# The opening of an FFT-and-MLP kernel: second twiddle table from two short series, bias parts made on eight partitions, weight loads first, three PSUM tiles for stage X

## The chip, the cores and the metric

The kernel runs on one core of one Trainium2 chip. The metric is device time in microseconds (us), as a median of several runs. The engines are TensorE (PE, with its weight loads shown as PEld), VectorE (DVE), ScalarE (ACT), GpSimd (POOL) and SyncE (SP), which issues most DMAs. POOL issues some DMAs as well. In the profile, queue q0 holds the DMAs that POOL issues and q1 those that SP issues.

## The reference

The input x has shape (8, 3008, 256). Each batch goes through a real FFT along the sequence, a complex linear layer with bias, a soft threshold, and the inverse FFT. The result goes through an MLP with an ELU.

```python
X = np.fft.rfft(x, axis=1)
Yr = Xr @ w_r - Xi @ w_i + b_r
Yi = Xr @ w_i + Xi @ w_r + b_i
Yr = np.sign(Yr) * np.maximum(np.abs(Yr) - 0.01, 0.0)      # the same for Yi
y = np.fft.irfft(Yr + 1j * Yi, n=3008, axis=1)
h = y.reshape(8 * 3008, 256) @ moe_w_in                    # 256 -> 2048
g = np.where(h > 0.0, h, np.exp(np.minimum(h, 0.0)) - 1.0)
out = g @ moe_w_out                                        # 2048 -> 256
```

## The kernel before

The FFT length is split as 3008 = 47 x 64. Each batch passes five stages on TensorE:

- A (`unit_A`, L129): six units, each the product of table M1 with 512 KB of x; the results are cast to bf16 and written to a DRAM buffer DA, because the next stage needs another layout.
- X (`unit_X`, L166): Z is loaded from DA in four pieces of eight rows (`load_Z`, L159). Eight units, two for each piece of Z, multiply with table M2. Each unit's result is copied ("evacuated") from PSUM to XT by `evac` (L123), on ACT (L127) or DVE (L125).
- M (`m_group`, L185): XT times the weights wcat_r and wcat_s. Half of batch 0's groups (`first_M` with on_act, L220) add the bias with one more matmul, of ones (busy) and bias_p. Rows 0, 32 and 64 of bias_p hold the bias as three bf16 parts that add up to its fp32 value. The other groups add bias_bc on DVE (L202) and are clipped on POOL (L230, L231).
- B (`unit_B`, L233) and Y (`unit_Y`, L274): the inverse, with tables M3 and M4, through a DRAM buffer DB, whose content comes back as Bs (`load_Bs`).

Batch 0 runs through these stages alone. From then on the MLP runs in a loop over blocks (`front` and `back`; L716 and L774 are its two products) with the stages of the next batches spread through it by `plan` (L801).

The tables M1 to M4 are computed on the chip, in the opening, beside stage A of batch 0. The order of instructions is written out by hand (`tc.manual_schedule()`), and each engine, and each DMA queue's issuer, works through its own list in order.

M2 holds cosines and sines of angles for 32 slots s of 2 x 24 columns on 96 partitions. The kernel before makes it in four groups g of eight slots (384 elements on each partition): `points` (L429) reduces integers mi to sample points kv and their half sign st; `phases` (L445) scales the points to angles v2; `wraps` (L460) takes the nearest integer away; `sizes` (L472) takes the absolute value on ACT; `signs` (L466) forms the second argument; `sines` (L476) is the Sin on ACT. `slot0` (L482) corrects slot 0.

The bias parts are made in place: six small DMAs put the two bias rows three times each into brow (L304), and full-width instructions on ACT and DVE split them (L601 to L610).

The weights w_r and w_i are loaded by SP after stage A's writes (L518, L519), and POOL arranges them in wcat_r and wcat_s, one part negated (L520 to L523). On SP the four Z loads, two loads of bias_bc (L527) and the first piece of w_in (L578) follow.

x for batch 0 comes in six loads (`first_x`, L314), issued by POOL between its iotas. `gate` (L585) is a small POOL copy that holds POOL until a piece of Z has landed, so that the loads of batch 1's x (L116) start only then.

`idle_pe(n)` (L295) issues n filler matmuls into a PSUM tile of their own (ips, L298): nine at the start, three between the A units, forty ahead of X, one after each X unit.

[...] In the opening pre2 has two tiles of two banks, used by A, X and B, pre1 three of one bank for M, and pre0 one for the fillers.

The functions that the change touches, and their callers:

## Time and profile before

| what | us |
|---|---|
| median of 3 runs | 912.17 (911.17 to 912.38) |
| the profiled execution | 911.1 |
| its span | 909.3 |
| first A matmul / last A matmul starts | 5.98 / 13.22 |
| last evacuation of A ends on ACT | 14.97 |
| Z is issued | 18.26 |
| first X matmul starts | 22.62 |
| last X evacuation ends | 30.69 |
| batch 1's first A matmul starts | 46.99 |
| first MLP product (L716) starts | 56.89 |

Times inside the execution count from the start of the span. The page of the profile gives each engine's busy time and a chain: the work that ended last, followed back through whatever released each step. The timeline lists instructions by start, duration, engine, line and operation; in brackets stands the idle time before and what ended it. The view of waits adds up who waited for whom. The DMA view counts the packets, bytes and busy share of each queue in a stretch of time. For the share, 100% is all 16 DMA engines busy.

### The profile page before, as it was taken

How to read it: one execution, taken by the hardware profiler on the slowest of the kernel's cores; microseconds unless marked ns; L12 is line 12 of the kernel's file. 1: busy time of each engine (PE TensorE's matmuls, PEld its weight loads, DVE VectorE, ACT ScalarE, POOL GpSimd, SP SyncE). 2: the span in 40 equal slices, each digit the busy share in tenths (PEclk: the TensorE clock that was granted, in tenths of full speed). 3: DMA queues.
4: the chain of work that ended last, by engine and by line, in shares of the span. 5: the costliest groups of instructions: out<-in, count | busy, mean ns of one | idle time of the engine just before them, and what ended most of it. 6: DMA issues, size and time to landing. Idle time of an engine off the chain costs nothing.

```text
span 909.3 us, 17183 instructions
## 1 busy us (share of the span) xinstructions
PE 887.7 (98%) x6622; PEld 652.0 (72%) x6726; DVE 717.0 (79%) x891; ACT 696.6 (77%) x851; POOL 314.7 (35%) x440
## 2 busy tenths in 40 slices
PE   8889999999999999999999999999999999999997
PEld 3457667876688677886678766787667866777775
DVE  8768778877788778797788877888778877778776
ACT  6668788777878778787787788878887877767664
POOL 7600540333321441405404153033332134443664
PEclk9999999999999999999999999999999999999999
DMA  8997116621283215732166032752228111231011
GB/s 270 309 265 232 47 48 186 209 70 47 83 236 123 71 47 142 192 109 82 58 196 199 24 98 60 207 171 70 70 70 232 29 43 47 79 86 48 24 48 47
DMA packets 90670, 106.24 MB, mean 117 GB/s; under 512 B 5270, under 2 KB 81308, under 8 KB 87228
## 3 DMA queue, kind: packets, MB, share of 16 engines
q1 hardware_dynamic: 84332, 77.62, 30.7%
q0 software_dynamic: 5968, 27.26, 9.1%
q8 instruction: 52, 0.85, 0.4%
q14 instruction: 30, 0.25, 0.1%
q10 hardware_dynamic: 288, 0.26, 0.1%
HBM read 55.32 MB, written 49.81 MB: 116 GB/s over the span
## 4 chain that ended last, share of the span: by engine, by line
PE 85%; DVE 5%; ACT 4%; DMA 3%; issue 2%; SPq 1%; POOL 0%; DVEq 0%; ACTq 0%; POOLq 0%
PE ps_o L774 34%; PE hps L716 33%; PE mps L192 9%; PE yps L282 2%; PE bps L244 2%; PE aps L144 2%; PE xps L175 2%; DMA Bs<-DB 2%; DVE gT L743 1%; DVE Et L755 1%; ACT Et L730 1%; ACT Et L727 1%; ACT Bz L257 1%; DVE osb L785 1%; SPq L792 0%
## 5 line engine op out<-in xcount | busy, mean ns | idle before, releaser
L774 PE MATMUL ps_o<-w_out_r,gT 128*128 128x256 f32 x3008 | 477.1, 301 | 0.2 <-DVE gT L741 0.2
L774 PEld LDWEIGHTS ps_o<-w_out_r,gT 128*128 128x128 f32 x3008 | 403.4, 189 | 50.3 <-DVE osb L785 1.3
L716 PE MATMUL hps<-yT,w_in_s 128*128 128x512 bf16 (+7 forms) x1650 | 382.1, 351 | 6.3 <-DVE gT L743 0.9
L741 DVE SCALAR_TENSOR_TENSOR gT<-Et,hps 128x512 fp32r<-128x512 f32 (+1 forms) x274 | 224.0, 847 | 75.8 <-POOL Et L753 38.8
L743 DVE SCALAR_TENSOR_TENSOR gT<-hps,Et 128x1024 fp32r<-128x1024 f32 x197 | 240.9, 1223 | 16.6 <-PE hps L716 1.4
L716 PEld LDWEIGHTS <-w_in_s 128*128 128x128 bf16 x1728 | 141.6, 98 | 129.0 <-issue 22.0
L730 ACT ACTIVATE Et<-hps 128x1024 f32<-128x1024 f32 x197 | 203.0, 1030 | 11.9 <-PE hps L716 5.4
L753 POOL TENSOR_SCALAR Et<-Et 128x512 f32<-128x512 f32 x189 | 112.5, 613 | 221.4 <-ACT Et L725 221.4
L755 DVE TENSOR_SCALAR Et<-Et 128x1024 f32<-128x1024 f32 x197 | 136.2, 691 | 47.4 <-ACT Et L730 40.5
L210 POOL TENSOR_SCALAR clip<-yb 128x512 f32<-128x512 f32 x84 | 51.6, 614 | 315.4 <-DVE yb L202 277.9
L725 ACT ACTIVATE Et<-hps 128x512 f32<-128x512 f32 x190 | 103.2, 595 | 64.7 <-PE hps L716 63.9
L727 ACT ACTIVATE Et<-hps 128x1024 f32<-128x1024 f32 x84 | 86.2, 1026 | 71.7 <-PE hps L716 70.1
L211 POOL TENSOR_TENSOR Y<-yb,clip 128x512 bf16<-128x512 f32 x84 | 107.2, 1276 | 7.0
L728 ACT ACTIVATE Et<-Et 128x1024 f32<-128x1024 f32 x84 | 88.8, 1058 | 2.7
L202 DVE TENSOR_TENSOR yb<-mps,bias_bc 128x512 f32<-128x512 f32 x89 | 61.3, 689 | 35.8 <-PE mps L192 23.9
L127 ACT CAST XT<-xps 128x768 bf16<-128x768 f32 x61 | 48.7, 799 | 16.2 <-PE xps L175 16.2
L127 ACT CAST yT<-yps 128x752 bf16<-128x752 f32 x63 | 49.7, 788 | 13.4 <-PE yps L282 13.3
L192 PE MATMUL mps<-wcat_r,XT 128*128 128x512 bf16 x180 | 55.6, 384 | 0.8 <-ACT Bz L257 0.3
L192 PE MATMUL mps<-wcat_s,XT 128*128 128x512 bf16 x182 | 54.9, 379 | 0.7
L127 ACT CAST A<-aps 128x1024 bf16<-128x1024 f32 x43 | 43.5, 1014 | 13.0 <-PE aps L144 12.3
L192 PEld LDWEIGHTS <-XT 128*128 128x128 bf16 x384 | 30.8, 98 | 29.6 <-DVE XT L125 0.6
L257 ACT CAST Bz<-bps 128x1024 bf16<-128x1024 f32 x46 | 46.0, 999 | 2.1 <-PE bps L244 2.1
(112 smaller groups left out, 413.5 us busy)
## 6 DMA issues: line engine op xcount, KB each, us to landing
xt<-in_x_dram POOLq DMA_DIRECT2D x21, 1024.0 KB, 7.2
out_dram<-osb SPq DMA_DIRECT2D x158, 128.0 KB
Bs<-DB SPq DMA_DIRECT2D x32, 384.0 KB
DB<-Bz SPq DMA_DIRECT2D x21, 512.0 KB
DA<-A SPq DMA_DIRECT2D x19, 512.0 KB
Z<-DA SPq DMA_DIRECT2D x7, 1152.0 KB
Z<-DA SPq DMA_DIRECT2D x11, 384.0 KB
xt<-in_x_dram POOLq DMA_DIRECT2D x6, 512.0 KB, 5.8
```

The source lines that it names most:

```text
L127: nc.scalar.copy(dst, src)
L192: nc.tensor.matmul(ps, lhsT=XT[:, dt, c, o : o + P], rhs=wm[:, dt, :], start=(not biased and m == 0 and dt == 0), stop=(m == 1 and dt == 1),)
L211: nc.gpsimd.tensor_tensor(Y_of[b, q][:, i, :], yb, clip[:], ALU.subtract)
L716: nc.tensor.matmul(hps[:, s, c0:c1], lhsT=w_in_s[:, dt, ft * P : ft * P + P], rhs=yT_of[b][:, dt, t0 : t0 + c1 - c0], start=(dt == 0), sto ...
L725: nc.scalar.activation(E_[:, s], hps[:, s], AF.Exp)
L727: nc.scalar.activation(E_, hps[:], AF.Relu, scale=-1.0)
L730: nc.scalar.activation(E_, hps[:], AF.Exp)
L741: nc.vector.scalar_tensor_tensor(o, e, -1.0, h, ALU.add, ALU.max)
L743: nc.vector.scalar_tensor_tensor(o, h, 0.0, e, ALU.max, ALU.add)
L753: eng.tensor_scalar(E_[:, s], E_[:, s], 1.0, 0.0, ALU.min, ALU.max)
L755: nc.vector.tensor_scalar(E_, E_, 1.0, -1.0, ALU.min, ALU.add)
L774: nc.tensor.matmul(po[q][:, i_ % 2, :], lhsT=gT[:, s, i_ * P : i_ * P + P], rhs=w_out_r[:, ft, :], start=(ft == 0 and i_ % 2 == 0), stop=( ...
```

## The change

It has four parts, all in the opening.

1. M2's angles. The integer points and their scaling are replaced by sums: a short series over the slots (sp, 32 elements) and a table over 78 offsets (tab). The table is read through a sliding window (`window`), which steps backward over the slots. A second table, tsg, gives the signs through the same window. `wraps` becomes one instruction, since a sum lies within one turn of the wanted range. The work goes in two halves of 16 slots, and slot 0's extra row reads tab directly. All sums and wraps stand ahead of stage A's evacuations on DVE, `sizes` and the first `sines` after unit 3 on ACT, `signs` after unit 5.
2. Bias parts. The bias is loaded as 8 x 64 by two DMAs and split by five small DVE instructions (`split_bias`) after the signs. The three parts are written to a DRAM buffer bias_d, ahead of the Z loads on SP, and read back into rows 0, 32 and 64 of bias_p, behind bias_bc. POOL clears bias_p early.
3. Weights and x. The loads of w_r and w_i become SP's first, and x's first load POOL's first. The negated part of wcat_s is made on ACT after the Sines. Unit 4 of stage A is emptied by DVE; unit 5 half by ACT and half by DVE, with a write for each half.
4. Stage X. It gets a pool of three two-bank PSUM tiles, closed before M; pre2 and pre1 are opened after it. DVE empties five of the eight units, ACT three; Abs and the two Sin of M3 go on ACT between them. The first M group takes both products of XT's first half before those of the second. The gate for batch 1's x waits for Z's fourth piece instead of its second. Fillers: 7 at the start instead of 9, 34 before X instead of 40, one after every other X unit.

```diff
@@ pools
-    pre2 = first.enter_context(tc.tile_pool(name="pre2", bufs=2, space=bass.MemoryType.PSUM))
-    pre1 = first.enter_context(tc.tile_pool(name="pre1", bufs=3, space=bass.MemoryType.PSUM))
     pre0 = first.enter_context(tc.tile_pool(name="pre0", bufs=1, space=bass.MemoryType.PSUM))
+    sooner = ExitStack()
+    pre2 = sooner.enter_context(tc.tile_pool(name="preX", bufs=3, space=bass.MemoryType.PSUM))
@@ unit_A
+        j0 = 8 * ci
+        if alone and u == 5:
+            for j in range(2):
+                c = 4 * uu + 2 * j
+                evac(A[:, c : c + 2, :].rearrange("p n d -> p (n d)"), ps[:, j, :], bool(j))
+                nc.sync.dma_start(dav[:, j0 + c : j0 + c + 2, :], A[:, c : c + 2, :])
+            return
@@ m_group
+        for n_ in range(4):
+            c, dt = (n_ % 2, n_ // 2) if (b, q, i) == (0, 0, 0) else (n_ // 2, n_ % 2)
...
@@ start
-    nc.vector.memset(brow[:], 0.0)
-    for o, bv in ((0, b_r), (D, b_i)):
-        for k in range(3):
-            nc.sync.dma_start(
-                brow[32 * k : 32 * k + 1, o : o + D],
...
-    idle_pe(9)
+    BR, BC = 8, 2 * D // 8
+    bpart = wk3.tile([BR, 3, BC], BF16, name="yb", tag="yb")
+    bias_d = dram.tile([3, BR, BC], BF16, name="bias_d", tag="bias_d")
...
+    first_x(0)
+    idle_pe(7)
+    def split_bias():
+        nc.vector.tensor_copy(bpart[:, 0], brow[:])
+        nc.vector.tensor_tensor(rest[:], brow[:], bpart[:, 0], ALU.subtract)
+        nc.vector.tensor_copy(bpart[:, 1], rest[:])
+        nc.vector.tensor_tensor(rest[:], rest[:], bpart[:, 1], ALU.subtract)
+        nc.vector.tensor_copy(bpart[:, 2], rest[:])
...
+        nc.sync.dma_start(w_r_f[:], w_r.rearrange("(c p) e -> p c e", p=P))
+        nc.sync.dma_start(w_i_f[:], w_i.rearrange("(c p) e -> p c e", p=P))
+        for o, bv in ((0, b_r), (BR // 2, b_i)):
+            nc.sync.dma_start(
+                brow[o : o + BR // 2, :],
...
@@ tables
+        def window(t, s0, ns, c, b):
+            return bass.AP(
+                tensor=t.tensor, offset=t[0:RZ, TD - s0 : TD - s0 + 1].offset,
+                ap=[t[0:RZ].ap[0], [-1, ns], [1 - 2 * c, K1]],
+            )
+        def short_tables():
+            dve.tensor_scalar(tmp[:], trow, 36.0 / N1, CMAGIC, ALU.mult, ALU.add)
...
+            dve.tensor_scalar(tsg[:], tji[:], NS + 0.5, -0.5, ALU.is_gt, ALU.add)
+        def sums(s0, s1):
+            for c in range(2):
+                dve.tensor_tensor(
+                    kt(v2, s0, s1)[:, :, :, c],
+                    sp[z, s0:s1].unsqueeze(2).to_broadcast([RZ, s1 - s0, K1]),
+                    window(tab, s0, s1 - s0, c, None), ALU.add,
+                )
...
+        def wraps(s0, s1):
+            v = v2[z, s0:s1]
+            dve.scalar_tensor_tensor(v, v, 0.5, v, ALU.is_gt, ALU.subtract)
+        def signs(s0, s1):
+            for c in range(2):
+                a = kt(a2, s0, s1)[:, :, :, c]
                 dve.scalar_tensor_tensor(
+                    a, a, qd[z], window(tsg, s0, s1 - s0, c, None), ALU.subtract, ALU.mult
                 )
@@ order
+            unit_A(0, u, alone=True, on_dve=u == 4)
...
+        short_tables()
+        sums(0, 16)
+        wraps(0, 16)
+        sums(16, 32)
+        wraps(16, 32)
+        for u in range(6):
             fA(u)
+            if u == 3:
+                sizes(0, 16)
+                sizes(16, 32)
+                sines(0, 16, 0)
+        signs(0, 16)
+        signs(16, 32)
+        split_bias()
+        nc.sync.dma_start(bias_d.rearrange("k r c -> r k c"), bpart[:])
         for g in range(4):
             load_Z(0, 8 * g, 8 * g + 8)
...
+        for k in range(3):
+            nc.sync.dma_start(
+                bias_p[32 * k : 32 * k + 1, :], bias_d[k : k + 1].rearrange("k r c -> k (r c)")
+            )
+        pool.tensor_copy(wcat_r[:, :, 0:D], w_r_f[:])
+        pool.tensor_copy(wcat_r[:, :, D : 2 * D], w_i_f[:])
+        pool.tensor_copy(wcat_s[:, :, D : 2 * D], w_r_f[:])
+        sines(16, 32, 0)
+        sines(0, 16, 1)
+        sines(16, 32, 1)
+        slot0()
+        nc.scalar.activation(wcat_s[:, :, 0:D], w_i_f[:], AF.Copy, scale=-1.0)
...
-        idle_pe(40)
+        idle_pe(34)
+        for u in range(8):
+            unit_X(0, u, alone=True, on_dve=u not in (0, 3, 6))
+            if u == 0:
+                nc.scalar.activation(a3[:], w3[:], AF.Abs)
+            if u in (3, 6):
+                o, src, sc, bi = ((1, w3, TURN, 0.0), (0, a3, -TURN, hpi[:]))[u // 6]
...
+            if u % 2 == 0:
+                idle_pe(1)
@@ after X
-    gate(Z_of[0][:, 8, 0:1])
+    gate(Z_of[0][:, 24, 0:1])
...
+    sooner.close()
+    pre2 = first.enter_context(
+        tc.tile_pool(name="pre2", bufs=2, space=bass.MemoryType.PSUM, reuse_waits="tile")
+    )
+    pre1 = first.enter_context(
+        tc.tile_pool(name="pre1", bufs=3, space=bass.MemoryType.PSUM, reuse_waits="tile")
+    )
```

## The prediction

> **What bounds the kernel now.** The page's engine table and chain come first: over the whole span TensorE is the bound.

> ```profile
> PE 887.7 (98%) x6622; PEld 652.0 (72%) x6726; DVE 717.0 (79%) x891; ACT 696.6 (77%) x851; POOL 314.7 (35%) x440
> PE 85%; DVE 5%; ACT 4%; DMA 3%; issue 2%; SPq 1%; POOL 0%; DVEq 0%; ACTq 0%; POOLq 0%
> ```

> The diff touches only work ahead of the first weight product, about the first 31 us of 909.3, where TensorE mostly runs filler (ips). So the question is when stage M of batch 0 can start. From there to 47 us the chain is nearly all TensorE, and what follows moves along with it. The chain of waits around that point:

> ```profile
> 24.93 0.88 DVE XT L125
> 25.80 0.04 issue
> 25.85 0.51 PE xps L175 x8
> ...
> 29.72 0.97 DVE XT L125
> 30.69 0.05 issue
> 30.73 0.82 PE mps L192 x3
> ```

> Stage M starts at 30.73, when DVE has emptied the last X unit. Two things set that: when Z arrives, and how fast eight X units pass two PSUM buffers. The latter is slow because DVE, which takes three of them, also splits the bias (timeline, DVE):

> ```profile
> 23.83 1.10 DVE L602 TENSOR_TENSOR yb<-yb,bias_p 128x512 f32<-128x512 f32 x1
> 24.85 0.94 DVE L125 CAST XT<-xps 128x768 bf16<-128x768 f32 x1
> 25.83 0.42 DVE L607 CAST bias_p<-yb 32x512 bf16<-32x512 f32 x1
> 26.26 0.42 DVE L608 CAST bias_p<-yb 64x512 bf16<-64x512 f32 x1
> 26.71 0.69 DVE L609 TENSOR_TENSOR yb<-yb,bias_p 64x512 f32<-64x512 f32 x1
> 27.44 0.69 DVE L610 CAST bias_p<-yb 64x512 bf16<-64x512 f32 x1
> ```

> Ahead of X lie transfers. The DMA view of 7.75 to 11.25 us shows x (q0) alone on the DMA engines, though three DA writes had been issued; from 11.25 to 17 the DA writes (q1) follow:

> ```profile
> q0 software_dynamic: 349, 1.26, 110.1%
> ...
> q1 hardware_dynamic: 3145, 1.57, 93.2%
> ```

> (packets, MB, share.) All six x loads land in turn and each stage-A pair of matmuls starts at a landing: 5.98, 7.16, 8.97, 10.37, 11.63, 13.22. Z is issued at 18.26, when the last DA write has landed (SP's waits, then its timeline):

> ```profile
> SPq L164 <- DMA DA<-A: 1.6, 1, 1.6
> ...
> 15.41 0.54 SPq L518 DMA_DIRECT2D w_r_f<-in_w_r_dram  x1
> 15.99 0.49 SPq L519 DMA_DIRECT2D w_i_f<-in_w_i_dram  x1
> 18.26 1.74 SPq L164 DMA_DIRECT2D Z<-DA  x4
> ```

> Counting 4 KB packets in windows of 0.25 us, Z's 384 are done at about 25.9; x landings came 0.55 to 1.05 after their last packets, so the last piece lands 8.2 to 8.7 us after Z's issue.

> **Weights first.** The w loads leave the place behind the DA writes and go out at about 0.75, when SP is released, instead of 15.41. Their 0.52 MB took 1.3 us at the rate of 17.25 to 18.55. That now lies ahead of x. In return x's first load goes out 0.65 sooner (1.47 now, behind five small POOL instructions) and the w packets fill part of the slow start (2.75 to 4.25). Bounds for x5: 0.65 earlier if the weights are free, 0.65 later if nothing overlaps; I take 0.3 later, since 1.3 us of data against 0.65 plus some start-up is nearer to the second. M1 keeps its time: DVE waited for the 0.48 memset, now gone, about as long as pcol is now pushed back by the load. Seven fillers instead of nine at the start cost nothing: x0 is awaited.

> **Second table.** Now DVE makes points, phases, wraps and signs in 384-element pieces, some 0.35 to 0.6 each, ending at 21.1, and POOL writes mi (0.91 + 0.83 + 1.0). After: nine small DVE instructions of 78 or fewer elements (0.25 each, from the 64-element rows of 0.21 to 0.28), four sums (0.55, L434), two 768-element wraps (0.9, L600), ready at about 12.2. What counts is the tail. After evacuation 3 (ends 12.12 now, 12.4 with the shift) ACT does two Abs and a Sin of 768 before it empties half of unit 5: three steps of 0.75 (the pitch of L613), so that half starts at 14.55 and ends at 15.15 (0.59, L254). DVE empties the other half, behind it; the one such split in this trace runs in series:

> ```profile
> 47.09 0.59 ACT L254 CAST A<-bps 128x512 bf16<-128x512 f32 x1 [0.31 <-PE bps L244]
> 47.71 0.69 DVE L255 CAST A<-bps 128x512 bf16<-128x512 f32 x1 [1.10 <-ACT A L254]
> ```

> So DVE is done at 15.86, 0.9 later than ACT is now (14.97). Behind that on DVE stand four signs (0.53, the pitch of L468): 17.95; then five instructions of split_bias (8x64; 0.22 by the 128x64 rows): 19.05.

> **Bias parts.** The new write to bias_d stands ahead of Z on SP and waits for split_bias. With 0.35 for its issue, Z goes out at 19.4, 1.15 later than now. The DA landing, the wait that ends last today, comes at about 18.5 (17.0 data end, 0.3 shift, 1.2 to land), so it loses its place to the new wait. Bounds of Z's issue: 18.5, the DA landing alone; 20.4, with x 0.65 later and small instructions at 0.3. I take 19.4, since it is a sum of rows of the same shapes.
> In return 3.3 us of DVE (L602 to L610) and 0.6 of ACT leave stage X, and 0.48 of memset the start. The three bias_p loads queue behind Z and bias_bc; they land by about 29 and are wanted at E + 0.5 (E: the end of the last X evacuation).

> **Three buffers and the M3 sines.** Evacuations go 5 to DVE (0.9 pitch) and 3 to ACT (0.8); Abs and two Sin (0.84, 0.85, 0.92) fit between. X alone would need 5.7 us against 8.1 now. Z's last piece, at 19.4 + 8.4 = 27.8, ends later than that pace from Z's first, landed by some 23.6 (23.6 + 5.7 = 29.3 against E below). From 27.8: 0.57 to the second unit, 0.51 matmuls, 0.04, 0.96 evacuation: E = 29.9 against 30.69, a gain of 0.8. Z lands late next, no longer DVE.

> **First M group reordered.** Both dt = 0 products go ahead of E, so two instead of three follow: 0.22 gained (matmul pitch 0.216).

> **At nothing.** The negated weights move from POOL (3.09, L522) to ACT (0.6), done near 19.3 under Z's transfer. The gate on Z piece 24 moves batch 1's x issue from 24.97 to about 28.2; it is read at 46.99 and took 8 to 11 us, so some 7 us of cover are left. POOL, idle 4.5 us before L230 today, is then free at about 31.3, wanted at E + 1.7 = 31.6; past that, the first B group has 0.4 in hand and the excess would be paid in full.

> **Sum.** -0.8 - 0.22 = -1.0 us on the profiled 911.1 (span 909.3 plus 1.8 around it): 910.1. The median of the runs lies 1.07 above that execution, so 912.17 - 1.0 = 911.1. Bounds: Z at 18.5, landing 8.1 later, gives E = 28.7, -2.2 in all; Z at 20.4 with 8.7 gives E = 31.2, +0.3.

> [...] Fillers in front of X fall from 40 to 34 and end near 21.4, while Z comes near 23.5: 2.1 us of idle TensorE, where 1.24 (before 25.85) is the longest gap in this opening. The nine first fillers take 4.02, 0.447 each, later ones 0.216, so a slow start exists here; that an idle gap brings it back no row shows. By the sum it costs nothing; if it came back in stage M, some 4 us at half pace would cost 2.0. [...]

> **Rivals.**
> 1. *All upstream is early.* The weights hide in x's start-up, DVE's small instructions are shorter, and Z goes out at 18.6 and lands 8.1 later: E = 28.8, -2.1, 910.1. For it: DMA moves little before 4 us. Against: signs and split_bias cannot begin before the half on DVE ends.
> 2. *Window reads are slow (slower).* sums and signs read a 78-element table with backward or overlapping steps. At 1.06 instead of 0.53, the sums end at 14.3, the half of unit 5 at 17.1, signs and split at 22.5, Z at 22.8, E = 33.3: +2.4, 914.6. It turns to a loss from about 0.8 each. For it: L487, 24 stepped elements, 0.35 against 0.18 for L439. Against: L434 with a repeated operand took 0.55 like the plain ones.
> 3. *The clock falls* (above): +1.0, 913.2.
> 4. *The bias does not get small in time:* its way through DRAM lands after E + 0.5. Each us late is paid; the six small loads of today needed about 3 us under x's traffic. At 2 to 4 late: 913 to 915.

> **How the numbers follow.** A change under 0.2% (1.8 us) is about what a measurement of this kernel can't tell from none. My forecast 0.45 (911.1; own range 910.0 to 912.4), 0.08 of it beyond -1.8; rival 1 0.34, 0.32 of it beyond; rival 2 0.11; rival 3 0.05, within; rival 4 0.05, 0.03 of it beyond on the slow side. Faster 0.08 + 0.32 = 0.40, slower 0.11 + 0.03 = 0.14, same 0.46. The range takes rival 1 with a margin of 0.7 below, and above it the bounds and rival 3: 909.4 to 913.4.

> **What would show it.** DVE idle until ACT's half of unit 5 ends, near 15.2; bias_d issued near 19.1 and Z right behind, SP waiting for split_bias and not for DA; X units 4 and 6 waiting for Z and not for a buffer; E near 29.9; from there to 47 the same row of products. I am wrong if Z goes out by 18.5, if the X units wait for DVE, or if products after E run slower than 0.216.

## The result and the profile after

The changed kernel takes 914.88 us (912.87 to 916.88) against 912.27 (910.76 to 914.30) for the kernel before on the same chip: a ratio of 1.0025, interval 1.0015 to 1.0035, so slower by 1.4 to 3.2 us. The forecast was 1.0 us faster. The profiled execution took 915.0 us, with a span of 913.2.

On the page of the changed kernel TensorE is still the bound. In the row of the granted clock (40 slices of 23 us, in tenths, 9 for 90% or more) the second slice is at 8, and in the chain DMA has 4% instead of 3.

```profile
PE 887.9 (97%) x6611; PEld 654.4 (72%) x6714; DVE 713.5 (78%) x888; ACT 691.6 (76%) x840; POOL 310.4 (34%) x435
...
PEclk9899999999999999999999999999999999999999
...
PE 85%; DVE 4%; DMA 4%; ACT 3%; issue 2%; SPq 0%; DVEq 0%; POOL 0%; ACTq 0%; POOLq 0%
```

The chain of waits of the changed kernel ahead of stage M (start, duration, what) goes back from M through X and Z to the bias parts:

```profile
19.53 1.06 DVE a L488 x2
20.58 0.11 DVE yb L322
...
21.42 0.19 DVE yb L326
21.62 0.02 issue
21.63 0.30 SPq L537
...
22.17 0.32 SPq L170
22.50 0.05 issue
22.55 6.14 DMA Z<-DA
...
33.75 0.97 DVE XT L125
34.72 0.14 issue
34.86 1.02 PE mps L198 x4
```

Stage M starts at 34.86 instead of 30.73. Z is issued at 22.17 instead of 18.26, 3.91 us later, and that is nearly all of it: from Z's issue to M it is 12.69 us, before 12.47. The three PSUM tiles brought nothing in this execution, in which X ran at half clock (below). SP's waits up to 24 us (total, times, longest) name what was ahead of Z: not the landing of stage A's writes, but split_bias.

```profile
SPq L161 <- ACT A L127: 11.4, 4, 7.2
SPq L537 <- DVE yb L326: 2.7, 1, 2.7
```

The timeline of VectorE shows why the bias parts came so late. Signs and split took what the forecast gave them (0.53 each; 0.17 to 0.21 each), but the half of unit 5 ahead of them started at 17.78, after a wait for ACT:

```profile
15.20 1.22 DVE L125 CAST A<-aps 128x1024 bf16<-128x1024 f32 x1 [2.53 <-PE aps L144]
17.78 0.69 DVE L125 CAST A<-aps 128x512 bf16<-128x512 f32 x1 [1.36 <-ACT A L127]
18.39 2.19 DVE L488 SCALAR_TENSOR_TENSOR a<-a,c,tsg 96x384 f32<-96x384 f32 x4
20.51 0.17 DVE L322 CAST yb<-yb 8x64 bf16<-8x64 f32 x1
```

And ACT was late for TensorE, whose timeline begins, first in the kernel before, then in the changed one:

```profile
1.45 4.02 PE L298 MATMUL ips<-busy 128*128 128x512 bf16 x9 [1.45 <-DVE busy L292]
5.98 0.72 PE L144 MATMUL aps<-xt,M 128*128 128x512 f32 x2 [0.51 <-DMA xt<-in_x_dram]
6.54 0.82 PE L298 MATMUL ips<-busy 128*128 128x512 bf16 x3
```

```profile
1.45 3.17 PE L304 MATMUL ips<-busy 128*128 128x512 bf16 x7 [1.45 <-DVE busy L298]
7.41 1.19 PE L144 MATMUL aps<-xt,M 128*128 128x512 f32 x2 [2.79 <-DMA xt<-in_x_dram]
8.40 1.50 PE L304 MATMUL ips<-busy 128*128 128x512 bf16 x3
9.34 1.42 PE L144 MATMUL aps<-xt,M 128*128 128x512 f32 x2
...
26.63 0.82 PE L181 MATMUL xps<-M,Z 96*128 96x96 bf16 x8 [2.99 <-DMA Z<-DA]
```

TensorE starts at half pace in both kernels: the first fillers begin 0.43 us apart, later ones 0.22. The kernel before is at full pace from 6.0 on, just when x0 (the first load of x) is there. In the changed kernel the seven fillers end at 4.62, x0 is there only at 7.41, and the half pace of the start lasts until 12.7: up to then a pair of matmuls on x takes 1.2 to 1.4 us instead of 0.70 to 0.74, and three fillers 1.50 instead of 0.82. The last pair starts at 15.47 instead of 13.22. Then the 34 fillers end at 23.64, Z comes at 26.63, and X runs at half clock too. The windows of the changed kernel (busy time of each engine; the last three numbers are granted clock, DMA share and GB/s) show the half clock of X. The 1.00 over stage A is no full clock: the packed trace's first record of the clock is at 12.74; the three fillers from 10.56 on took 1.50, the three from 12.71 on 0.84.

```profile
0.00:16.00 16.00, 11.76 (x34) 5.19 (x34) 10.77 (x40) 6.72 (x9) 13.29 (x40) 1.00 0.84 279
...
26.60:30.00 3.40, 3.15 (x29) 2.40 (x30) 1.36 (x2) 1.54 (x2) 0.00 (x0) 0.50 1.02 239
30.00:33.00 3.00, 2.78 (x33) 2.64 (x33) 2.14 (x3) 1.54 (x2) 0.82 (x2) 0.50 0.77 235
```

So three suspects stood beside each other: the weights ahead of x, too few fillers, and the bias write ahead of Z.

### The profile page after: what moved, and what is told of

The parts are those of the page before. It is cut to its first block, busy times and chain, and to the rows that moved or that the text cites. A ratio compares the mean times of both kernels' runs of the same rounds, so it can differ in the third digit from the quotient of the medians.

```text
span 913.2 us, 17139 instructions
## 1 busy us (share of the span) xinstructions
PE 887.9 (97%) x6611; PEld 654.4 (72%) x6714; DVE 713.5 (78%) x888; ACT 691.6 (76%) x840; POOL 310.4 (34%) x435
## 3 DMA queue, kind: packets, MB, share of 16 engines
q1 hardware_dynamic: 84390, 77.62, 30.4%
## 4 chain that ended last, share of the span: by engine, by line
PE 85%; DVE 4%; DMA 4%; ACT 3%; issue 2%; SPq 0%; DVEq 0%; POOL 0%; ACTq 0%; POOLq 0%
PE ps_o L781 34%; PE hps L723 33%; PE mps L198 9%; PE yps L288 2%; PE bps L250 2%; PE xps L181 2%; PE aps L144 2%; DVE gT L750 2%; DMA Bs<-DB 2%; DVE Et L762 1%; ACT Et L737 1%; ACT Et L734 1%; ACT Bz L263 1%; DMA Z<-DA 1%; DMA xt<-in_x_dram 1%
## 5 line engine op out<-in xcount | busy, mean ns | idle before, releaser
L737 ACT ACTIVATE Et<-hps 128x1024 f32<-128x1024 f32 x197 | 202.9, 1030 | 11.8 <-PE hps L723 5.2
L127 ACT CAST A<-aps 128x1024 bf16<-128x1024 f32 (+1 forms) x42 | 42.2, 1004 | 15.8 <-PE aps L144 14.2
L198 PEld LDWEIGHTS <-XT 128*128 128x128 bf16 x384 | 30.8, 98 | 29.9 <-ACT M L575 1.3
```

The lines of the kernel that those rows point to most:

```text
L127: nc.scalar.copy(dst, src)
L198: nc.tensor.matmul(ps, lhsT=XT[:, dt, c, o : o + P], rhs=(wcat_r, wcat_s)[c][:, dt, :], start=(not biased and n_ == 0), stop=n_ == 3,)
L737: nc.scalar.activation(E_, hps[:], AF.Exp)
```

## The experiments

All medians and marks in one table; the sections below use it. "vs before" is the difference to the median of the kernel before, measured beside it on the same chip (912.27 with 16 executions for the changed kernel; 912.44, 912.35, 911.94 and 912.27 us with 29 to 35 for the four groups of experiments). The ratio is a second estimate of the same; in best2 the two are 2.0 and 1.3 us. Its interval reaches 0.7 to 1.4 us to each side, so two versions whose intervals overlap are not told apart by it. The marks come from one profiled execution each: the first record of TensorE's clock in the packed trace, from which on it ran at full pace; start of the matmuls on x0 and x5 (the first and last load of x); Z's issue; the time from there until the last piece of Z was seen to have landed (by the X unit or the POOL gate that waited for it; in brackets by the trace's landing records, where nothing waited for it or the wait does not stand out); the first product behind the last X evacuation; and stretches with a granted clock of about 0.5 between 2 and 66 us.

| kernel | median | vs before | ratio, interval | full pace | x0 | x5 | Z | landing | M | half clock |
|---|---|---|---|---|---|---|---|---|---|---|
| before | | | | 6.0 | 5.98 | 13.22 | 18.26 | (8.6) | 30.73 | none |
| changed | 914.88 | +2.6 | 1.0025 [1.0015, 1.0035] | 12.7 | 7.41 | 15.47 | 22.17 | 9.6 | 34.86 | 26.4-33.4 |
| f_start | 913.48 | +1.0 | 1.0011 [1.0001, 1.0021] | 4.4 | 7.34 | 14.17 | 20.05 | 9.5 | 32.59 | 28.2-38.6 |
| f_mid | 913.93 | +1.5 | 1.0017 [1.0004, 1.0029] | 13.2 | 7.11 | 15.51 | 22.22 | 9.3 | 34.91 | 30.2-33.8 |
| f_both | 913.98 | +1.5 | 1.0017 [1.0008, 1.0026] | 6.8 | 8.01 | 13.65 | 20.36 | 9.5 | 32.13 | none |
| f_both_zfirst | 912.72 | +0.3 | 0.9999 [0.999, 1.0009] | 6.8 | 8.00 | 13.65 | 18.62 | 9.5 | 30.34 | 58.0-61.6 |
| a_wlate | 914.31 | +2.0 | 1.003 [1.0016, 1.0043] | 10.1 | 5.59 | 14.28 | 20.34 | 9.6 | 32.47 | 30.6-37.6 |
| b_wfirst | 913.33 | +1.0 | 1.0013 [1.0002, 1.0024] | 5.0 | 6.82 | 13.68 | 18.47 | (9.0) | 31.09 | none |
| b_gate24 | 911.23, one execution | | | 9.8 | 6.08 | 13.34 | 19.33 | 8.7 at most | 31.55 | none |
| best | 910.73 | -1.6 | 0.9989 [0.998, 0.9997] | 5.5 | 5.55 | 14.01 | 18.34 | 9.8 | 30.39 | none |
| best_wfirst | 909.69 | -2.3 | 0.9975 [0.9965, 0.9985] | 5.1 | 7.07 | 13.83 | 18.35 | 8.8 | 29.41 | none |
| best_few | 911.85 | -0.1 | 0.9999 [0.9984, 1.0014] | 5.0 | 5.28 | 14.26 | 18.57 | (10.1) | 31.00 | 25.4-29.0 |
| best_biaslate | 911.78 | -0.2 | 0.9997 [0.9988, 1.0006] | 6.7 | 5.40 | 14.11 | 19.82 | 9.3 | 31.29 | none |
| b_warm | 913.63 | +1.7 | 1.0015 [1.0006, 1.0025] | 4.7 | 5.57 | 13.76 | 18.97 | (8.4) | 32.12 | none |
| a_warm | 913.37 | +1.1 | 1.0009 [0.9997, 1.002] | 10.4 | 6.84 | 14.05 | 20.76 | 10.1 | 33.29 | 27.4-31.0 |
| a_early | 912.28 | 0.0 | 1.0 [0.9989, 1.0011] | 13.4 | 7.20 | 15.69 | 20.65 | 9.1 | 32.22 | 30.4-37.4 |
| best2 | 910.30 | -2.0 | 0.9986 [0.9977, 0.9994] | 6.4 | 7.07 | 14.06 | 18.53 | 9.3 | 30.04 | none |

### Fillers, and the bias write behind Z

```diff
 f_start:         -    idle_pe(7)          +    idle_pe(19)
 f_mid:           -        idle_pe(34)     +        idle_pe(48)
 f_both:          both
 f_both_zfirst:   both, and
-        nc.sync.dma_start(bias_d.rearrange("k r c -> r k c"), bpart[:])
         for g in range(4):
             load_Z(0, 8 * g, 8 * g + 8)
+        nc.sync.dma_start(bias_d.rearrange("k r c -> r k c"), bpart[:])
```

> The changed kernel with 19 fillers at the start instead of 7, so that TensorE has work until x's first load lands. Theory C (clock): with TensorE idle from 4.62 to 7.41 the clock is granted at half, so that fillers and A matmuls set stage A's pace (2.16 us a unit); with the gap filled, stage A follows the x landings again, the fourth A unit is emptied by about 12.3 instead of 15.07, Z is issued near 19.4 instead of 22.2, and the time falls by 2 to 4 us. Theory T (transfers only): x's first load lands late behind the weights, the rest follows from it and from the DVE tail, fillers do nothing: Z near 22, time as the changed kernel's (about 914.9).

> The changed kernel with 48 fillers ahead of X instead of 34, nothing else. Theory C: Z is still issued near 22.2, but no X matmul runs at half clock (unit 0.51 instead of 0.82), stage M starts 0.5 to 1 us sooner than 34.9, the time falls by 0.5 to 1. Theory T: no change.

> Both filler counts raised (19 and 48). Theory C: the forecast's course comes out: Z at about 19.4, stage M at about 30.0 to 30.5, time 0.5 to 1.5 us below the kernel before. Theory T: about 914.9.

> As both filler counts raised, and the write to bias_d stands behind the four Z loads on SP instead of ahead of them. Theory C with the forecast's step (the write waits for split_bias on DVE, Z behind it): Z issued at the landing of the last DA write, about 18.5 instead of 19.4, 0.9 us less than with both counts raised. If that step is false: the same as with both counts raised.

With TensorE busy until x0, full pace comes at 4.4, stage A follows x again and Z goes out at 20.05, 2.1 sooner. By the medians f_start gains 1.6 of the 2.6 lost, where theory C had 2 to 4, and f_mid 1.1, where it had 0.5 to 1; both intervals overlap that of the changed kernel. Against theory C, M came no sooner in f_mid's profiled execution: the clock fell behind gaps of 1.02 and 0.49 within stage X. f_both is the telling one, a miss for both theories: TensorE was at full pace from 6.8 on and never lost its clock, and it is still 1.5 us slower than before, with M at 32.13. So half pace isn't the whole loss. Its chain goes from the signs through split_bias and the bias write to Z:

```profile
16.57 2.19 DVE a L488 x4
...
19.61 0.19 DVE yb L326
19.80 0.02 issue
19.82 0.30 SPq L537
...
20.36 0.32 SPq L170
...
21.66 8.21 DMA Z<-DA
```

Moving that one write behind Z brings Z forward by 1.74, M by 1.79 and, on the same chip, the median by 1.3.

### The weights

```diff
 a_wlate (from the changed kernel):
-        nc.sync.dma_start(w_r_f[:], ...)      # SP's first
-        nc.sync.dma_start(w_i_f[:], ...)
         for u in range(6):
             fA(u)
+        nc.sync.dma_start(w_r_f[:], ...)
+        nc.sync.dma_start(w_i_f[:], ...)
 b_wfirst (from the kernel before): the two loads SP's first, first_x(0) POOL's first
 best (from the changed kernel): the edit of a_wlate, and
         wraps(16, 32)
+        split_bias()
         for u in range(6):
             fA(u)
+            if u == 4:
+                nc.sync.dma_start(bias_d.rearrange("k r c -> r k c"), bpart[:])
...
-    idle_pe(7)
+    idle_pe(10)
-        idle_pe(34)
+        idle_pe(40)
-            if u % 2 == 0:
-                idle_pe(1)
+            idle_pe(1 if u < 7 else 3)
-    idle_pe(6)      # ahead of stage Y
+    idle_pe(8)
```

> The changed kernel with the two weight loads put back behind stage A's writes on SP; nothing else, so still 7 and 34 fillers and the bias write ahead of Z. If the weights are what delays x: x0 lands near 5.8 as in the kernel before (7.27 in the changed kernel), TensorE's wait for it shrinks from 2.79 to about 1.2, stage A's matmuls run at 0.70 to 0.74 a pair from the second unit on and follow x's landings, Z is issued near 19.2 (changed 22.17), and the median falls from 914.9 to 912.7 or so (the wait for the bias parts and Z's landing 9.5 us after its issue stay). If the weights cost no more than the 0.3 that the prediction gave them, and x0 was late for POOL's start, x0 lands at 7 or later and the time stays within 0.5 of 914.9.

> The kernel before with the weight loads SP's first and x's first load POOL's first; the rest as before (9 and 40 fillers, two PSUM tiles, large bias parts). If weights first is what costs: x0 lands near 7.2 instead of 5.84, the idle time of TensorE ahead of it is 2 us or more, the first A units run slowly, x5 lands 0.7 to 1.3 later, Z is issued 19.0 to 21 (before 18.26) and the median rises by 0.8 to 3 us over the kernel before. If weights first is free, as rival 1 had it, x5 lands no later, Z is issued at 18.3 or sooner, and the median stays within 0.4 of the kernel before.

> The changed kernel with what the runs speak against undone: the weights behind stage A's writes, split_bias right behind the wraps and its write on SP behind unit 4's, so that nothing but stage A's writes and the two weight issues stands ahead of Z; 10 fillers at the start, 40 ahead of X, one behind every X unit and three behind the last, 8 ahead of stage Y. If Z's issue is what sets stage M: Z near 18.3, its last piece near 27.8, the last X evacuation near 29.8, M near 29.9 (before 30.73), and the time 0.5 to 1 below the kernel before, 911.4 to 911.9. If the signs alone already hold DVE or Z lands later still, M starts at 30.7 or later and the time is that of the kernel before within 0.4.

With the weights late x0 comes at 5.59, as the first theory said, and yet the time stays at 914.3, much as the second did. The profiled execution has the half pace of the start until 10.1 and half clock from 30.6. And in the variants of the changed kernel x5 is no later with the weights first: 13.65 to 14.17 where TensorE had full pace by x0, 14.01 to 14.28 with the weights late. In the kernel before, weights first costs 1.0 us (0.2 to 2.2 by the interval), but its one profiled execution was the fastest of its twelve (911.3), and so doesn't show where. best is the first version below the kernel before, by 1.6 us (0.3 to 1.8 by the interval), with Z at 18.34 as expected, released by the landing of stage A's write.

### How long Z takes in the kernel before

```diff
 b_gate24 (from the kernel before):
-    gate(Z_of[0][:, 8, 0:1])
+    gate(Z_of[0][:, 24, 0:1])
```

> The kernel before, with the gate for batch 1's x on Z's fourth piece instead of its second, so that POOL's wait shows when that piece lands. If Z takes 8.2 to 8.7 from issue to its last landing, as the prediction read from the packets, POOL is released at 26.5 to 27.0 (issue at 18.26). If it takes 9.5 as in the runs of the changed kernel, at 27.8: then stage X of the kernel before ended by Z too and not by DVE's evacuations alone.

POOL's timeline of this kernel:

```profile
28.03 0.24 POOL L588 CAST gate<-Z 96x1 f32<-96x1 bf16 x1 [2.83 <-ACT XT L127]
```

Z was issued at 19.33, so its last piece was there no later than 8.70 after its issue: the 8.2 to 8.7 that the prediction read from the packets holds for the kernel before, where the landing records have 8.6 (8.4 in b_warm, 9.0 in b_wfirst). In the changed kernel and its variants it was 8.8 to 10.1. What lengthens it wasn't settled. This execution also shows that the kernel before can keep the half pace of the start well into stage A: 1.19 and 1.42 for a pair of matmuls, until 9.8.

### One part of best undone, and fillers alone

```diff
 best_wfirst:    best with the weight loads SP's first again
 best_few:       best with 7, 34, one after every other X unit, and 6 fillers again
 best_biaslate:  best with split_bias behind the signs and its write ahead of Z again
 b_warm (from the kernel before):
-    idle_pe(9)
+    idle_pe(10)
-        idle_pe(1)      # behind each X unit
+        idle_pe(2 if u < 7 else 3)
-    idle_pe(6)
+    idle_pe(8)
```

> The best version so far (weights behind stage A's writes, bias parts early, more fillers; 910.7) with the weight loads put back as SP's first; all else stays. If they push x back as in the changed kernel: x0 lands near 7.2 instead of 5.5, TensorE idles 1.2 to 1.5 us ahead of it, x5 lands 0.5 to 1 later, Z goes out at 18.8 to 19.3 (best 18.34) and the median rises by 0.5 to 1.5 us. If it is TensorE's pace alone that mattered, and 10 fillers are enough, the median stays within 0.3 of best.

> The best version with the changed kernel's numbers of fillers (7 at the start, 34 ahead of X, one behind every other X unit, 6 ahead of stage Y) and nothing else changed. If few fillers are what lets TensorE fall to half pace: a gap of 1 us or more ahead of x0 and of 1.5 to 2.5 us ahead of X, half pace in stage A or a granted clock of 0.5 between 23 and 60 us in most executions, and the median 1.5 to 3 us above best, 912.2 to 913.7. If the order of the transfers alone mattered, it stays within 0.4 of best.

> The best version with split_bias and its write back where the changed kernel has them: split behind the signs, the write on SP ahead of the Z loads. If that wait sets Z: SP's bias write near 19.3 to 19.6, Z near 19.8 to 20.1 instead of 18.34, stage M 1.3 to 1.7 later, the median 1 to 1.7 us above best, 911.7 to 912.4. If the landing of stage A's last write sets Z as well, as the kernel before has it, Z moves by less than 0.3 and the median by less than 0.4.

> The kernel before with more fillers alone: 10 instead of 9 at the start, two instead of one behind each X unit and three behind the last, 8 instead of 6 ahead of stage Y. If the fillers alone are what the best version gains over the kernel before, the median falls by 1 us or more, to 911.4 or below. If the kernel before seldom loses its clock, it stays within 0.4 of 912.3, and the gain of the best version comes from the tables and the bias.

best_wfirst is a miss that clears the suspect: weights first isn't slower but, if anything, faster (909.69, all eight executions within 909.17 and 910.15). x0 comes at 7.07 behind a gap of 1.50, but full pace has come at 5.1, so the pairs take 0.70 to 0.74; Z goes out as in best, and its last piece lands 1.0 sooner. SP's waits and the chain of best_wfirst show what sets Z now, as in the kernel before:

```profile
SPq L170 <- DMA DA<-A: 1.4, 1, 1.4
```

```profile
16.35 1.88 DMA DA<-A
18.23 0.02 SPq L170
...
18.35 0.32 SPq L170
...
19.65 7.49 DMA Z<-DA
27.15 0.05 issue
27.19 0.53 PE xps L181 x8
...
27.75 0.80 ACT XT L127
28.54 0.84 ACT M L576
...
29.41 0.59 PE mps L198 x2
```

best_few costs 1.1 in the median (1.5 by the distances to the kernel before), which is less than expected and not clear of the noise, and spreads from 908.8 to 915.1 where best stays within 909.3 to 912.6. The granted clock, which is on record for every execution, goes with it: 1.000 in the fastest of best_few, 0.991 to 0.993 in its four slowest, 0.998 or 0.999 in all of best. So few fillers don't cost every time. best_biaslate is much as expected: Z 1.48 later, the median 1.1 (1.5 by the distances), M only 0.90; here too the intervals overlap. b_warm is a miss: more fillers alone make the kernel before 1.7 slower. It lost no clock; in its profiled execution M was 1.4 later, 0.7 of it because Z was, and 0.7 in stage X, where two fillers stood behind each unit of a stage that waits for its evacuations. Why Z was later stays open. So best's gain over the kernel before is not the fillers alone.

### The two edits, one at a time

```diff
 a_warm:   the changed kernel with best's fillers
 a_early:  the changed kernel with split_bias behind wraps(16, 32), its write behind unit 4's
 best2:    both; the same kernel as best_wfirst
```

> The changed kernel with more fillers alone: 10 at the start, 40 ahead of X, one behind every X unit and three behind the last, 8 ahead of stage Y. If TensorE's half pace is the larger loss: the pair of matmuls on x stays at 0.70 to 0.74, no granted clock below 1 in the opening, Z near 19.9 to 20.4 (changed 22.17) since the wait for the bias parts is still there, stage M near 31.4 to 32, a narrow spread, and a median near 911.5 (best_wfirst 909.7 plus 1.5 to 2 for the wait). If the wait is the larger loss, it stays at 913 or above.

> The changed kernel with split_bias right behind the wraps and its write on SP behind unit 4's, nothing else: still 7 and 34 fillers. If fillers and wait add up (wait 1.5 to 2, fillers 3 to 3.5): the median falls to 913 or so, with a spread of 4 us or more, and Z goes out right after the landing of stage A's last write, at 18.3 where TensorE keeps its pace and at 20.3 or so where stage A runs at half pace. If the wait was all that mattered, the median falls to 910.5 or below.

> Both edits again, the same kernel as best_wfirst: if its gain is real, 909.7 within 0.3, and a ratio to the kernel before of 0.997 to 0.998.

The weights are first in all, and the three were measured on one chip, the changed kernel's +2.6 on its own: fillers alone bring it to +1.1, the early bias write alone to 0.0, both to -2.0 (-2.3 in best_wfirst). best2 missed the 909.7 within 0.3 that was expected: 910.30, the ratio 0.9986. The two gains, 1.5 and 2.6, add up to 4.1 against 4.6 measured. By the medians the wait is the larger, more than the first theory of a_early gave it; as the intervals of a_warm and a_early overlap, that order is not shown. Nor did a_warm keep TensorE's pace as its first theory had it. Its timeline:

```profile
1.45 4.45 PE L304 MATMUL ips<-busy 128*128 128x512 bf16 x10 [1.45 <-DVE busy L298]
6.84 1.19 PE L144 MATMUL aps<-xt,M 128*128 128x512 f32 x2 [0.95 <-DMA xt<-in_x_dram]
...
25.34 0.52 PE L181 MATMUL xps<-M,Z 96*128 96x96 bf16 x8 [1.82 <-DMA Z<-DA]
```

The half pace of the start lasted until 10.4 there; in best2, with the same fillers, it ended at 6.4. So best2 has full pace behind a longer gap ahead of x0, and with Z 2.2 sooner no gap ahead of X:

```profile
1.45 4.45 PE L304 MATMUL ips<-busy 128*128 128x512 bf16 x10 [1.45 <-DVE busy L298]
7.07 0.70 PE L144 MATMUL aps<-xt,M 128*128 128x512 f32 x2 [1.18 <-DMA xt<-in_x_dram]
...
23.25 0.51 PE L181 MATMUL xps<-M,Z 96*128 96x96 bf16 x8
```

With these fillers the early Z thus came with two gains: M starts at 30.04 instead of 33.29, and TensorE, which in a_warm waited 1.82 for Z and was at half clock from 27.4 to 31.0, has no such wait and no stretch at half clock.

## Why the prediction was wrong

The forecast had the sign wrong. Step by step:

- **"The new write to bias_d stands ahead of Z on SP and waits for split_bias"**: right, and so was that it takes the place of the landing of stage A's write. Its price was too low. Where TensorE had full pace early Z went out at 19.8 to 20.4 (best_biaslate, f_start, f_both), forecast 19.4, bound 20.4: split_bias ended at 19.5 in f_start, 0.4 late, and from the bias write to Z's issue it was 0.5 instead of 0.35. Without the wait it goes out at 18.35 to 18.6, forecast 18.5. So the wait is 1.5 to 1.8 where the sum had 0.9. (As written, three steps of 0.75 from 12.4 and four signs of 0.53 add up to 0.1 more than the sum took, which changes nothing.)
- **"Seven fillers instead of nine at the start cost nothing: x0 is awaited"**: this step failed. The prediction read the slow start off the first fillers and let it end with them. TensorE does wait for x0, but its half pace did not end with the fillers: with seven of them and a wait of 2.79 it lasted until 12.7; stage A then hung on TensorE and not on x. In the profiled execution that is 2.1 of the 3.9 by which Z was late (f_start). Full pace came before 7 us in one of the five profiled executions with seven fillers, in seven of nine with nine or ten, and in all three with nineteen.
- **Weights first, x5 0.3 later**: right in size for x5 (13.7 to 14.2 where full pace came early, against 13.2 to 13.8 in the kernel before, b_gate24 and b_warm). What was missed is x0, 1.4 later, which matters by the gap that it leaves on TensorE. The weights alone are no cause: best_wfirst, with them first, has the lowest median.
- **Three buffers**: the direction was right, the size not. From Z's issue to M the sum had 10.5 us against 12.5 before. With the clock kept up to M it was 11.1 to 11.5 (best_wfirst, best2, best_biaslate), 11.7 and 11.8 (f_both_zfirst, f_both) and 12.1 in best, so the gain is 0.4 to 1.4 instead of 1.9. The mis-sized term is the landing of Z's last piece, 8.8 to 10.1 after its issue instead of 8.4.
- **First M group reordered, 0.22 gained**: not seen. All four products follow the last evacuation (the x4 at 34.86 in the chain), where the sum had two and the kernel before three. M's PSUM tiles now come out of the pool that X has just left, which could hold the first product. So could the second Sin of M3, which the forecast put between the evacuations for nothing: the chain of best_wfirst names it ahead of M, 0.1 us behind the last evacuation. Both are argued, no run tried them.
- **The sum with both sizes mended** and the clock kept: Z 1.6 to 2.1 later, X 0.4 to 1.4 shorter, so 0.2 to 1.7 slower before any half pace; f_both, with full clock in its profiled execution, was 1.5 slower.
- **Rival 3, the clock falls**, was right that it does (half clock for 6.8 us from 26.4 on; X starts at 26.63), with a chance of 0.05 and a price that counted only stage M (2.0, so 1.0 in all). The sum counted 2.1 us of idle TensorE ahead of X at nothing, a term that no run shows; in the traces the longest gap in the 3.4 us ahead of the fall was 1.02 in f_mid, 1.15 in a_early, 2.75 in the changed kernel. Nor did the number of fillers settle when full pace comes: the three executions that have nine at the start came to it at 5.0 (b_wfirst), 6.0 (the kernel before) and 9.8 (b_gate24).
- **Rival 2, slow window reads**: refuted, sums and signs took 0.51 to 0.55 each. **Rival 1**: half of it holds, since x5 lost little to the weights, but its Z at 18.6 needs the wait gone. **Rival 4**: bias_p was never late; its product follows in place at 35.72 in the changed kernel.
- **POOL, the gate on Z's fourth piece and the negated weights at nothing**: no wait for them showed up in the chain.

## What to carry to other kernels

A small transfer put ahead of a large one on the same queue made the large one wait here for what the small one waited for: SP waited 2.7 us for split_bias, and with the bias write behind Z, Z went out 1.74 sooner. Ask of each queue what the moved transfer's input hangs on, since moving this one and what it waits for ahead in their lists was worth 2.6 us. Fillers that look spare because TensorE only waits anyway can matter to its pace: in the profiled executions full pace came at 12.7 with seven at the start and at 4.4 with nineteen (f_start), though at 5.0 with the seven of best_few. Count the busy share of TensorE over a few us around each gap, not the gap alone: it was 19 to 56% over the 3.4 us ahead of the eight falls of the clock, while the longest gap there was no more than 1.02 in f_mid. When a change bundles several edits, an unhappy result doesn't condemn them all: two small edits turned this one from 2.6 us slower into 2.0 to 2.3 us faster than the kernel before by the medians (1.3 to 2.3 by the ratios), with the suspected third, the weights first, kept.

## What the runs showed of the hardware

The windows of a_warm show such a stretch: 1.81 us busy of the 4 between 23 and 27, and a clock of 0.57 over the next 4:

```profile
15.00:23.00 8.00, 8.00 (x39) 3.62 (x38) 6.20 (x20) 4.29 (x7) 0.42 (x1) 1.00 0.42 114
23.00:27.00 4.00, 1.81 (x21) 0.87 (x19) 1.51 (x3) 1.11 (x2) 0.00 (x0) 1.00 1.01 273
27.00:31.00 4.00, 3.79 (x36) 2.96 (x37) 2.32 (x3) 1.97 (x3) 0.12 (x1) 0.57 1.00 251
```

- Ahead of full pace the clock column reads 1.00 though TensorE is at half pace: in the changed kernel it has 1.00 over 0 to 16 us, where the first record of the clock is at 12.74 and a pair of matmuls on x took 1.19 to 1.42 up to then. The pace of equal matmuls is the safer reading there.
- Two executions of nearly the same opening differ by a microsecond: b_gate24 issued Z at 19.33 and the kernel before at 18.26, with nothing changed ahead of it; the slow start lasted until 9.8 in the one and 6.0 in the other. Marks from one profile are no better than that, which is why the verdicts above rest on medians.
